# Fourteen more of block B's maximum reductions in the V stage, and the V rows stored from ScalarE's queue

## The chip, the cores and the metric

The kernel runs on one core of one Trainium2 chip. The metric is device time in microseconds (us) from launch to end, lower is better. Each kernel is run three times and the median counts; one more execution is profiled.

## The reference, cut to what matters

Two attention blocks over 2048 positions, width 640, 32 heads of 20 channels. Block A attends each position to 8 earlier positions at stride 2; block B is full softmax attention. The outputs stand side by side.

```python
def _B_ref(x, wqkv, wo):
    qkv = (x @ wqkv).reshape(B, S, 3, H, Dh).transpose(2, 0, 3, 1, 4)
    q, k, v = qkv[0], qkv[1], qkv[2]
    scores = jnp.einsum("bhqd,bhkd->bhqk", q, k) * (Dh ** -0.5)
    p = _softmax(scores, axis=-1)
    o = jnp.einsum("bhqk,bhkd->bhqd", p, v)
    return o.transpose(0, 2, 1, 3).reshape(B, S, D) @ wo
```

## The kernel before

The program is one long straight line of instructions. Its stages: block A's projections of q, k and v; block B's q and k projections; the **V stage**, block B's v projection; the **loop**, block B's attention; a tail without maxima; the last output projections. Block A's attention (pieces of GpSimd work, `a_attention`, line 350) runs under the later stages, one piece each time `next(a_work)` is called.

**PSUM.** One tile `ps_st` holds all 8 banks. `bank()` (line 115) hands out one bank, `wide()` (134) two neighbours. In the V stage banks 0 to 3 rotate for the projections, and the pairs 4-5 and 6-7 for the maxima. Inside the loop, `one` and `two` pick banks by estimated times while the order is written out.

**V stage** (lines 892 to 929). `V_GROUPS` has 32 groups, 30 of them here and the last two at the start of the loop. A group is 15 matmuls `128x320` into one bank (`rows15`, 263: weights `ww`, data `xn` and `xl`), a ScalarE copy into one of four row tiles `ve`, and a store of these rows to DRAM (`vb_d`). The store stands on SP's queue, one group later (`after(1, sp.dma_start, ...)`). Between the first groups SP also issues the loads of q (`bq`, four per group) on which the maxima rest, and after groups 8 and 16 loads of x.

**Maxima.** The softmax of block B needs each query's maximum over all keys before its exponentials. Work is counted in 512 *steps* (8 groups of 4 heads, 4 query blocks, 16 key blocks). One step of maxima is two halves; a half is a pair of matmuls (60 rows by 512 columns, side by side in the array, into a pair of banks: rows `ps_st<-bk,bq 60*128`) and a VectorE `tensor_reduce` of 128x1024. `b_max` (695) writes one step, and after groups 7 to 30 the V stage has one step each: 24 steps, `LEAD`. When 16 steps are done, `max_rows` (627) reduces and transposes them on VectorE and sends them into q's extra rows.

**Loop** (961 to 1015). Each `V` token ends a step: `begin` (DMA issues, block A's pieces) and `b_pv` (709: 8 recorded matmuls `ps_st<-e,vb` per step, and every second step a ScalarE copy). `S` writes two score halves (matmul `ps_st<-bq,bk 62*128`, ScalarE exponential of 128x512), `M` one half of maxima (two matmuls, one reduction of 1024), `Y` one score half beside half of a half of maxima (reduction of 512). The tokens stand in strings:

```python
PLAIN = "VYMSVYMSYY"                              # 2 steps, and 2 steps of maxima
MIXED = "VYMSVYjMYYFYMSYVYMSVYSMYVYkYSVMSY"       # 6 steps, block A's output piece at F
```

The loop runs 488 steps; its maxima are `LEAD` = 24 steps ahead, so the last 24 steps (the tail) have none. `i % 30 % 4 == 1` (line 974) says at which steps `i` below 240 block A takes its next piece.

Of the kernel before, what the change touches and what calls it, by code (L numbers as in the profile page):

```python
# [12 lines left out]
ALU = mybir.AluOpType  # L13
AX = mybir.AxisListType
# [10 lines left out]
VC = DH + 1  # L25
# [15 lines left out]
NKB = 16  # L41
NS = NG * NQC * NKB
LEAD = 24
LAG = 2
NEG = -1.0e30

# [19 lines left out]
def attention_pair(ctx, tc, xa, wqk_a, wv_a, wo_a, xb, wqk_b, wv_b, wo_b, oa, ob):  # L66
# [13 lines left out]
    def after(n, fn, *args):  # L80
        due.setdefault(now[0] + n, []).append((fn, args))
# [25 lines left out]

    psb = ps.tile([128, 8, 512], F32, name="ps_st")
    free = list(range(4))
    pair = [0]  # L110
    taken = {}
    read_at = []

# [19 lines left out]

    def wide():

        pair[0] += 1
        return psb[:, 4 + 2 * (pair[0] % 2):6 + 2 * (pair[0] % 2)]

    def one(t, *but):

# [48 lines left out]
    def chunk(t, xi, k):  # L189
        return t[k // (KC - 1)][:, xi, k % (KC - 1)]  # L190
# [69 lines left out]
        w = sb.tile([128, 2, KC, 128], F32R, tag="w", bufs=4, name="w")  # L260
        return w, [lambda: split(w[:, 0], w[:, 1], wqk_b[m])]

    def rows15(p, o, W):

        for k in range(KC):
            for i, (wi, xi) in enumerate(PASSES):
                pe.matmul(p[:, :320], o(xi, k), W[wi][:, k], start=(k == 0 and i == 0), stop=(k == KC - 1 and i == 2))

    def a_rows(p, x, t, g, W, ks, passes=PASSES):
        n = A_COLS[g + 1] - A_COLS[g]  # L270
# [402 lines left out]
    def max_tiles(i):  # L673
        u, sub = divmod(i, NKB)
        if sub == 0 and u not in mxt:
            mxt[u] = (sb.tile([128, 2, 8, 4], F32, tag="mx4", bufs=2, name="mx4"),
                      m1s[u % 2])
        return mxt[u]

    def m_matmul(i, j, r, p):  # L680

        u, sub = divmod(i, NKB)
        g, qc = divmod(u, NQC)
        q, k, v = stacks[g]
        pl, qb = divmod(sub // 2, 4)
        c = sub % 2 * 2 + j
        rows = slice(r * HALF, r * HALF + BS)
        pe.matmul(p, q[rows, qc, pl, qb * 128:qb * 128 + 128], k[rows, pl, c * 512:(c + 1) * 512], start=True, stop=True)

    def max_end(i):  # L690
        u, sub = divmod(i, NKB)
        if sub == NKB - 1:
            max_rows(*mxt[u], stacks[u // NQC][0], u % NQC)

    def b_max(i):

        m4 = max_tiles(i)[0]
        pq, ch = divmod(i % NKB, 2)
        for j in range(2):
            p = wide()  # L700
            for r in range(2):
                m_matmul(i, j, r, p[:, r])
            dve.tensor_reduce(m4[:, :, pq, 2 * ch + j], p, AX.X, ALU.max)
        max_end(i)

    P = {}
    accs, raws, spare = {}, {}, []
# [113 lines left out]
    def m_two():  # L821

        n = m_next[0]
        m_next[0] += 1
        max_tiles(n // 2 + LEAD)
        return "m", n // 2 + LEAD, n % 2

    def m_done(m):

# [59 lines left out]

    steps = iter(range(LEAD))
    WV = [WV, w1]
    groups = 0

    def v_group(n, half, s):
        p = bank()
        rows15(p, lambda xi, k: chunk(XB[n], xi, k)[:, s % 4 * 128:s % 4 * 128 + 128], WV[half])
        ve = ones[s % 4]
        act.copy(ve[:, :16 * VC].rearrange("p (h c) -> p h c", c=VC)[:, :, :DH],  # L900
                 p[:, :320].rearrange("p (h d) -> p h d", d=DH))
        give(p)
        c = 16 * VC + 11 * half
        after(1, sp.dma_start, vb_d[s * 128:(s + 1) * 128, half * 16 * VC:half * 16 * VC + c], ve[:, :c])


    V_GROUPS = [(n, half, s) for n in (2, 3, 0, 1) for half in range(2) for s in range(4 * n, 4 * n + 4)]
    v_late = V_GROUPS[-LAG:]
    for n, half, s in V_GROUPS[:-LAG]:
        v_group(n, half, s)  # L910
        tick()
        groups += 1
        if q_loads:
            for _ in range(4):
                q_loads.pop(0)()
        if groups == 1:
            wait[0] = 5
        if groups in (8, 16):
            XB[groups // 8 - 1], more = x_pieces(xb, groups // 8 - 1, gp)
            for fn in more:  # L920
                fn()
        if groups > 6:
            for i in islice(steps, 1):
                b_max(i)
        if groups > 16 and groups % 3 == 0 and groups != 21:
            next(a_work, None)
        if groups in (26, 28):
            v_piece(0, *((0, 4) if groups == 26 else (8, 16)))
# [31 lines left out]
    def begin(i):  # L960

        g, sub = divmod(i, NQC * NKB)
        if sub == 4 and g + 1 < NG:
            k_loads, q_loads = b_pieces(g + 1)
            for n, fn in enumerate(k_loads + q_loads + [lambda g=g + 1: v_piece(g, 0, NKB)]):
                after(1 + 2 * n, fn)
        if i in (NS - 56, NS - 40):
            out_first((i - NS + 56) // NKB)
        tick()
        if loads and i % 2:  # L970
            loads.pop(0)()
        if turn_jobs and turn_jobs[0][0] <= now[0]:
            run_jobs(turn_jobs, 1)
        if i > 14 and (i % 30 % 4 == 1 if i < 240 else i % 14 in (1, 5, 7, 11)):
            run_jobs(soft_jobs, 2)
            if next(a_work, 0) == 0:
                for d in done_a:
                    d[0] -= 1
        if done_a and done_a[0][0] <= 0:
            a_turn(*done_a.pop(0)[1:])  # L980
        turn_parts()


    PLAIN = "VYMSVYMSYY"
    MIXED = "VYMSVYjMYYFYMSYVYMSVYSMYVYkYSVMSY"
    i, order, mixed = 0, "", 0
    while i < NS - LEAD or order:
        if not order:
            if not left_a[0] and not WO_b:
                load_out(wo_b, WO_b)  # L990
            order = PLAIN
            if i + 6 <= NS - LEAD and ready_a and ready_a[0][0] <= now[0] + 3 and (
                    soft_jobs or next_a[0] == len(UNITS) or now[0] > max(mixed, ready_a[0][0]) + 14):
                order, mixed = MIXED, now[0] + 6
        kind, order = order[0], order[1:]
        if kind == "F":
            out_piece()
        elif kind == "j":
            run_jobs(*((soft_jobs, 1) if soft_jobs else (turn_jobs, 3)))
        elif kind == "k":  # L1000
            run_jobs(soft_jobs, 1)
            run_jobs(turn_jobs, KC)
        elif kind != "V":
            b_token(kind)
        else:
            begin(i)
            if i >= LAG:
                b_pv(i - LAG)
            else:
                v_group(*v_late.pop(0))  # L1010
                if not v_late:
                    load_out(wo_a, WO, (1,))

                    spare += [sb.tile([128, 2, 512], F32, tag="last0", bufs=2, name="more") for _ in range(2)]
            i += 1

    read_at.clear()
    for i in range(NS - LEAD, NS + LAG):
        begin(i)
        if i < NS:  # L1020
            b_qk(i)
        if i % 2:
            b_pv(i - LAG - 1)
            b_pv(i - LAG)
            if fill:
                fill.pop(0)()
# [57 lines left out]
```

## Time and profile before

| what | value |
|---|---|
| device time, median of 3 runs (lowest to highest) | 1791.26 us (1790.36 to 1794.95) |
| the profiled execution's own time / its span | 1788.76 us / 1787.0 us |
| granted TensorE clock, mean | 0.999 |
| busy share of the span: PE, PEld, DVE, ACT, POOL | 99%, 55%, 75%, 74%, 68% |
| V stage with maxima (364.9 to 437.0 us) | 24 steps of maxima |
| loop (437.0 to 1652.0 us) | 488 steps |

PE is TensorE's matmul, PEld its weight load, DVE VectorE, ACT ScalarE, POOL GpSimd, SPq the DMA issues of SyncE, ACTq those of ScalarE. A row of the timeline is one instruction or a run of equal ones: start, time from the start of the first to the end of the last, engine, line, operation, out<-in, count, and in brackets the idle time before it and what ended that. Neighbouring instructions overlap, so the distance between starts says more of their cost than their durations. Every row names line 61, the helper that records all instructions; names of tiles tell them apart.

### The profile page before, as it was taken

Reading aid. Unit: us, or ns where it says so; the run is one execution under the profiler, and the core shown is the slowest. Engines: PE = TensorE matmul, PEld = TensorE weight load, DVE = VectorE, ACT = ScalarE, POOL = GpSimd, SP = SyncE. Lnnn points to the kernel's source line nnn. Section 1 sums busy time; section 2 is a strip of 40 time slices with the busy share of each in tenths; the row PEclk is TensorE's granted clock in tenths of the full one; section 3 lists DMA queues with packets and bytes.
Section 4 is the critical chain, followed back from the end, with each engine's and each line's share of the span. In section 5 each row is a group of like instructions: output and inputs, shape, how many; then the busy total and the mean of one; then the engine's idle time right before and its main releaser. Section 6 shows DMA issues by size and latency. Waiting matters only on the chain. (4 is left out here: it accounts for less than half of the span.)

```text
span 1787.0 us, 31655 instructions
## 1 busy us (share of the span) xinstructions
PE 1772.1 (99%) x11211; PEld 987.1 (55%) x11211; DVE 1340.0 (75%) x1834; ACT 1327.2 (74%) x2593; POOL 1217.1 (68%) x1072
## 2 busy tenths in 40 slices
PE   9999999999999999999999999999999999999999
PEld 7988888887344444444444444444444434443469
DVE  3100232367999999999999999999999999999300
ACT  4222322222998999999999999998998998899881
POOL 0000069226679999989998999999999997337241
PEclk9999999999999999999999999999999999999999
DMA  6333696854535444354536336354444453113123
GB/s 228 116 100 102 190 304 245 270 187 139 152 88 148 124 136 120 106 151 133 147 99 170 96 113 163 121 159 130 133 142 124 122 149 94 30 44 86 32 70 114
DMA packets 191191, 240.22 MB, mean 134 GB/s; under 512 B 89020, under 2 KB 115260, under 8 KB 190040
## 3 DMA queue, kind: packets, MB, share of 16 engines
q1 hardware_dynamic: 190456, 237.54, 44.5%
q8 instruction: 88, 1.44, 0.4%
q14 instruction: 71, 0.58, 0.1%
q10 hardware_dynamic: 576, 0.66, 0.1%
HBM read 173.21 MB, written 64.91 MB: 133 GB/s over the span
## 5 line engine op out<-in xcount | busy, mean ns | idle before, releaser
L61 DVE TENSOR_REDUCE mx<-ps_st 128x1 f32<-128x512 f32 (+1 forms) x1512 | 1218.2, 871 | 57.7 <-PE ps_st L61 51.3
L61 ACT ACTIVATE e<-ps_st 128x512 f32<-128x512 f32 x2048 | 1066.2, 615 | 37.7 <-PE ps_st L61 16.4
L61 PE MATMUL ps_st<-bq,bk 62*128 62x512 f32 x2048 | 614.4, 436 | 1.4 <-DVE mx L61 0.6
L61 PE MATMUL ps_st<-bk,bq 60*128 60x512 f32 x2048 | 593.4, 446 | 3.9 <-DVE mx L61 2.1
L61 PEld LDWEIGHTS ps_st<-bq,bk 62*128 62x128 f32 x2048 | 283.0, 184 | 479.3 <-ACT e L61 282.3
L61 PE MATMUL ps_st<-e,vb 128*32 128x512 f32 x4096 | 543.7, 605 | 3.8 <-ACT e L61 2.6
L61 POOL TENSOR_TENSOR braw<-braw,more 128x512 f32<-128x512 f32 x224 | 287.8, 1285 | 136.5 <-ACT more L61 133.2
L61 POOL TENSOR_TENSOR akv<-akv,aq 128x1280 f32<-128x1280 f32 x64 | 189.0, 2953 | 234.4 <-DMA akv<-ka_d 234.4
L61 PEld LDWEIGHTS ps_st<-bk,bq 60*128 60x128 f32 x2048 | 267.7, 184 | 71.3 <-DVE mx L61 36.7
L61 POOL TENSOR_TENSOR akv<-akv 128x640 f32<-128x640 f32 (+3 forms) x304 | 282.2, 928 | 23.8
L61 ACT COPY ro<-ps_st 128x320 f32<-128x320 f32 (+2 forms) x124 | 61.2, 495 | 226.6 <-PE ps_st L61 177.2
L61 PEld LDWEIGHTS ps_st<-e,vb 128*32 128x32 f32 x4096 | 82.1, 108 | 158.8 <-ACT e L61 76.6
L61 POOL TENSOR_TENSOR akv<-akv,al 128x1280 f32<-128x1280 f32 x64 | 152.0, 2375 | 0.2
L61 ACT COPY more<-ps_st 128x512 f32<-128x512 f32 x224 | 133.4, 595 | 2.9 <-PE ps_st L61 2.7
L61 PE MATMUL ps_st<-wc,xn 128*128 128x512 f32 (+1 forms) x576 | 133.5, 376 | 0.4 <-ACT xn L61 0.4
L61 PE MATMUL ps_st<-ww,xn 128*128 128x320 f32 x768 | 125.8, 314 | 0.0
L61 PEld LDWEIGHTS ps_st<-ww,xn 128*128 128x128 f32 x768 | 113.4, 188 | 20.1 <-ACT ve L61 7.7
L61 PEld LDWEIGHTS ps_st<-wc,xn 128*128 128x128 f32 x576 | 106.2, 188 | 18.4 <-ACT xn L61 1.0
L61 PE MATMUL ps_st<-xn,w 128*128 128x512 f32 x480 | 115.7, 390 | 0.0
L61 PEld LDWEIGHTS ps_st<-xn,w 128*128 128x128 f32 x480 | 90.1, 188 | 19.4
L61 ACT CAST pr<-ps_st 128x512 fp32r<-128x512 f32 x40 | 23.5, 587 | 101.0 <-PE ps_st L61 101.0
L61 DVE TENSOR_TENSOR pr<-ps_st,pr 128x512 fp32r<-128x512 f32 x40 | 27.7, 692 | 91.7 <-ACT pr L61 91.7
(64 smaller groups left out, 986.0 us busy)
## 6 DMA issues: line engine op xcount, KB each, us to landing
akv<-ka_d SPq DMA_DIRECT2D x128, 320.0 KB
akv<-va_d SPq DMA_DIRECT2D x128, 320.0 KB
kb_d<-pr SPq DMA_DIRECT2D x20, 512.0 KB
qb_d<-pr SPq DMA_DIRECT2D x20, 512.0 KB
bk<-kb_d SPq DMA_DIRECT2D x16, 640.0 KB
bq<-qb_d SPq DMA_DIRECT2D x64, 160.0 KB
rb<-s_d SPq DMA_DIRECT2D x128, 64.0 KB
stg<-xb SPq DMA_DIRECT2D x12, 512.0 KB
```

The source lines that it names most:

```text
L61: return self.tc.keep_in_program_order(op(*a, **k))
```

## The change

1. `LEAD_0` = 31: the V stage computes 31 steps of maxima (62 halves) instead of 24 (48 halves), and the loop's maxima begin at step 31. They no longer stand between groups but inside them: `behind` is called after each of a group's matmuls, and three halves are written after matmul 105 of the stage and then after every 17th (21 places, the last with two halves).
2. PSUM: the maxima rotate over three pairs (2-3, 4-5, 6-7). The first six groups use banks 6, 4, 7, 5, 1, 0, and from group 7 on groups alternate between banks 1 and 0.
3. The V rows' store follows its copy at once on ScalarE's queue; the two late groups in the loop still use SP.
4. In the loop a third string, `LIGHT`, has 6 steps and 5 steps of maxima. It is taken in place of `PLAIN` seven times from step 16 on, wherever `MIXED` is not due, and brings the lead back from 31 to 24.
5. At step 61 block A's piece is left out; the pieces behind it all come one place later.

```diff
--- before.py
+++ after.py
@@ -41,6 +41,7 @@
 NKB = 16
 NS = NG * NQC * NKB
 LEAD = 24
+LEAD_0 = 31
 LAG = 2
 NEG = -1.0e30
 
@@ -107,7 +108,7 @@
 
     psb = ps.tile([128, 8, 512], F32, name="ps_st")
     free = list(range(4))
-    pair = [0]
+    pair, pairs_at = [0], [4, 2]
     taken = {}
     read_at = []
 
@@ -133,8 +134,9 @@
 
     def wide():
 
-        pair[0] += 1
-        return psb[:, 4 + 2 * (pair[0] % 2):6 + 2 * (pair[0] % 2)]
+        first, n = pairs_at
+        pair[0] = (pair[0] + 1) % n
+        return psb[:, first + 2 * pair[0]:first + 2 * pair[0] + 2]
 
     def one(t, *but):
 
@@ -260,11 +262,12 @@
         w = sb.tile([128, 2, KC, 128], F32R, tag="w", bufs=4, name="w")
         return w, [lambda: split(w[:, 0], w[:, 1], wqk_b[m])]
 
-    def rows15(p, o, W):
+    def rows15(p, o, W, behind=lambda n: None):
 
         for k in range(KC):
             for i, (wi, xi) in enumerate(PASSES):
                 pe.matmul(p[:, :320], o(xi, k), W[wi][:, k], start=(k == 0 and i == 0), stop=(k == KC - 1 and i == 2))
+                behind(3 * k + i + 1)
 
     def a_rows(p, x, t, g, W, ks, passes=PASSES):
         n = A_COLS[g + 1] - A_COLS[g]
@@ -692,16 +695,16 @@
         if sub == NKB - 1:
             max_rows(*mxt[u], stacks[u // NQC][0], u % NQC)
 
-    def b_max(i):
+    def b_max(i, j):
 
         m4 = max_tiles(i)[0]
         pq, ch = divmod(i % NKB, 2)
-        for j in range(2):
-            p = wide()
-            for r in range(2):
-                m_matmul(i, j, r, p[:, r])
-            dve.tensor_reduce(m4[:, :, pq, 2 * ch + j], p, AX.X, ALU.max)
-        max_end(i)
+        p = wide()
+        for r in range(2):
+            m_matmul(i, j, r, p[:, r])
+        dve.tensor_reduce(m4[:, :, pq, 2 * ch + j], p, AX.X, ALU.max)
+        if j:
+            max_end(i)
 
     P = {}
     accs, raws, spare = {}, {}, []
@@ -822,8 +825,8 @@
 
         n = m_next[0]
         m_next[0] += 1
-        max_tiles(n // 2 + LEAD)
-        return "m", n // 2 + LEAD, n % 2
+        max_tiles(n // 2 + LEAD_0)
+        return "m", n // 2 + LEAD_0, n % 2
 
     def m_done(m):
 
@@ -889,24 +892,39 @@
 
 
 
-    steps = iter(range(LEAD))
+    steps = iter(range(2 * LEAD_0))
     WV = [WV, w1]
     groups = 0
 
+    maxima_at = {7 * 15 + n * 17 for n in range(21)}
+
+    def maxima(n):
+        if groups * 15 + n in maxima_at:
+            for m in islice(steps, 3):
+                b_max(*divmod(m, 2))
+
     def v_group(n, half, s):
         p = bank()
-        rows15(p, lambda xi, k: chunk(XB[n], xi, k)[:, s % 4 * 128:s % 4 * 128 + 128], WV[half])
+        rows15(p, lambda xi, k: chunk(XB[n], xi, k)[:, s % 4 * 128:s % 4 * 128 + 128], WV[half], maxima)
         ve = ones[s % 4]
         act.copy(ve[:, :16 * VC].rearrange("p (h c) -> p h c", c=VC)[:, :, :DH],
                  p[:, :320].rearrange("p (h d) -> p h d", d=DH))
         give(p)
         c = 16 * VC + 11 * half
-        after(1, sp.dma_start, vb_d[s * 128:(s + 1) * 128, half * 16 * VC:half * 16 * VC + c], ve[:, :c])
+        dst = vb_d[s * 128:(s + 1) * 128, half * 16 * VC:half * 16 * VC + c]
+        if read_at:
+            after(1, sp.dma_start, dst, ve[:, :c])
+        else:
+            act.dma_start(dst, ve[:, :c])
 
 
     V_GROUPS = [(n, half, s) for n in (2, 3, 0, 1) for half in range(2) for s in range(4 * n, 4 * n + 4)]
     v_late = V_GROUPS[-LAG:]
+
+    free[:], pairs_at[:], pair[0] = [6, 4, 7, 5, 1, 0], [2, 3], 0
     for n, half, s in V_GROUPS[:-LAG]:
+        if groups == 6:
+            free[:] = [1, 0]
         v_group(n, half, s)
         tick()
         groups += 1
@@ -919,9 +937,6 @@
             XB[groups // 8 - 1], more = x_pieces(xb, groups // 8 - 1, gp)
             for fn in more:
                 fn()
-        if groups > 6:
-            for i in islice(steps, 1):
-                b_max(i)
         if groups > 16 and groups % 3 == 0 and groups != 21:
             next(a_work, None)
         if groups in (26, 28):
@@ -971,7 +986,7 @@
             loads.pop(0)()
         if turn_jobs and turn_jobs[0][0] <= now[0]:
             run_jobs(turn_jobs, 1)
-        if i > 14 and (i % 30 % 4 == 1 if i < 240 else i % 14 in (1, 5, 7, 11)):
+        if i > 14 and (i % 30 % 4 == 1 and i != 61 if i < 240 else i % 14 in (1, 5, 7, 11)):
             run_jobs(soft_jobs, 2)
             if next(a_work, 0) == 0:
                 for d in done_a:
@@ -981,9 +996,11 @@
         turn_parts()
 
 
+
     PLAIN = "VYMSVYMSYY"
+    LIGHT = "YYSVYYYVYMYSVYYYVSMSYVYMSVYY"
     MIXED = "VYMSVYjMYYFYMSYVYMSVYSMYVYkYSVMSY"
-    i, order, mixed = 0, "", 0
+    i, order, mixed, fewer = 0, "", 0, LEAD_0 - LEAD
     while i < NS - LEAD or order:
         if not order:
             if not left_a[0] and not WO_b:
@@ -992,6 +1009,9 @@
             if i + 6 <= NS - LEAD and ready_a and ready_a[0][0] <= now[0] + 3 and (
                     soft_jobs or next_a[0] == len(UNITS) or now[0] > max(mixed, ready_a[0][0]) + 14):
                 order, mixed = MIXED, now[0] + 6
+            elif i > 14 and fewer:
+                order = LIGHT
+                fewer -= 1
         kind, order = order[0], order[1:]
         if kind == "F":
             out_piece()
@@ -1015,6 +1035,7 @@
             i += 1
 
     read_at.clear()
+    free[:], pairs_at[:], pair[0] = [0, 1, 2, 3], [4, 2], 0
     for i in range(NS - LEAD, NS + LAG):
         begin(i)
         if i < NS:
```

**TensorE in the V stage, about the first maxima.** Before:

```order
L61 MATMUL ps_st<-ww,xl 128x320 x3
L61 MATMUL ps_st<-bk,bq 128x512 x4
L61 MATMUL ps_st<-ww,xn 128x320 x12
L61 MATMUL ps_st<-ww,xl 128x320 x3
L61 MATMUL ps_st<-bk,bq 128x512 x4
```

and now:

```order
L62 MATMUL ps_st<-ww,xl 128x320 x3
L62 MATMUL ps_st<-bk,bq 128x512 x6
L62 MATMUL ps_st<-ww,xn 128x320 x12
L62 MATMUL ps_st<-ww,xl 128x320 x3
L62 MATMUL ps_st<-ww,xn 128x320 x2
L62 MATMUL ps_st<-bk,bq 128x512 x6
L62 MATMUL ps_st<-ww,xn 128x320 x10
L62 MATMUL ps_st<-ww,xl 128x320 x3
L62 MATMUL ps_st<-ww,xn 128x320 x4
L62 MATMUL ps_st<-bk,bq 128x512 x6
```

Two halves after every 15 matmuls became three halves after every 17, so the places wander through the groups.

**SP's queue at the first loads of q.** The names in brackets are the semaphores that an instruction waits for; the eight DMAHW ones are shared by the DMAs of all queues in turn, and a DMA waits until the one that last counted on its semaphore has landed. Before:

```order
L61 DMA vb_d<-ve 128x336 [waits DMAHW4_49,Activation_49]
L61 DMA bq<-qb_d 20x1024 [waits DMAHW5_49,PE_49]
L61 DMA bq<-qb_d 40x1024 [waits DMAHW6_49]
L61 DMA bq<-qb_d 20x1024 [waits DMAHW7_49]
L61 DMA bq<-qb_d 40x1024 [waits DMAHW0_49]
L61 DMA vb_d<-ve 128x336 [waits DMAHW1_49,Activation_49]
```

and now, with the V rows' stores on ScalarE's queue:

```order
L62 DMA bk<-kb_d 22x4096 [waits DMAHW1_49]
L62 DMA bq<-qb_d 20x1024 [waits DMAHW3_49,PE_49]
L62 DMA bq<-qb_d 40x1024 [waits DMAHW4_49]
L62 DMA bq<-qb_d 20x1024 [waits DMAHW5_49]
L62 DMA bq<-qb_d 40x1024 [waits DMAHW6_49]
L62 DMA bq<-qb_d 20x1024 [waits DMAHW7_49]
```

SP no longer waits for ScalarE here. But semaphores 4, 5 and 6, for which the second to fourth load of q wait, are now those of the stores of V groups 3, 4 and 5 on ScalarE's queue.

**VectorE in the loop** (128x1 is a reduction of 512, 128x2 one of 1024; the number behind `mx` is a buffer's). Before, in `PLAIN` steps:

```order
L61 TENSOR_REDUCE mx_3488<-ps_st 128x1
L61 TENSOR_REDUCE mx_3488<-ps_st 128x2
L61 TENSOR_REDUCE mx_3488<-ps_st 128x1 x3
L61 TENSOR_REDUCE mx_3488<-ps_st 128x2
L61 TENSOR_REDUCE mx_3488<-ps_st 128x1
```

and now, in a `LIGHT` stretch:

```order
L62 TENSOR_REDUCE mx_3756<-ps_st 128x1
L62 TENSOR_REDUCE mx_3756<-ps_st 128x2
L62 TENSOR_REDUCE mx_3756<-ps_st 128x1 x4
L62 TENSOR_REDUCE mx_3756<-ps_st 128x2
L62 TENSOR_REDUCE mx_3756<-ps_st 128x1 x2
L62 TENSOR_REDUCE mx_3756<-ps_st 128x2
L62 TENSOR_REDUCE mx_3756<-ps_st 128x1 x8
```

Per 2 steps there were 2 wide and 4 narrow reductions; per 6 steps there are now 3 wide and 14 narrow instead of 6 and 12.

## Rows read from the trace of the kernel before

**Rows 1.** The page, busy time and share of the span by engine.
```profile
PE 1772.1 (99%) x11211; PEld 987.1 (55%) x11211; DVE 1340.0 (75%) x1834; ACT 1327.2 (74%) x2593; POOL 1217.1 (68%) x1072
```
**Rows 2.** Busy time in stretches: the V stage, and five of the loop.
```profile
core 0: us, PE busy (x) PEld busy (x) DVE busy (x) ACT busy (x) POOL busy (x), PEclk, DMA share, GB/s
366.58:436.98 70.40, 70.40 (x438) 57.54 (x437) 54.92 (x50) 15.55 (x32) 37.89 (x32) 1.00 0.52 155
...
463.65:477.86 14.21, 14.13 (x96) 5.74 (x96) 14.18 (x19) 13.81 (x28) 7.67 (x8) 1.00 0.54 159
544.66:566.99 22.33, 22.33 (x154) 8.90 (x154) 22.21 (x33) 21.70 (x44) 21.39 (x23) 1.00 0.63 175
477.86:536.55 58.69, 57.68 (x385) 23.45 (x384) 58.55 (x82) 55.64 (x110) 46.88 (x37) 1.00 0.31 88
552.86:566.99 14.13, 14.13 (x97) 5.86 (x96) 14.01 (x18) 13.77 (x28) 13.58 (x13) 1.00 0.59 162
582.93:611.77 28.84, 28.34 (x194) 11.61 (x192) 28.54 (x37) 28.02 (x57) 27.58 (x28) 1.00 0.37 108
```
**Rows 3.** The second stretch of the loop, the value matmuls alone.
```profile
544.66:566.99 22.33, 10.56 (x80) 1.48 (x80) 1.00 0.63 175
```
**Rows 4.** Timeline of PE and DVE about one V group with maxima.
```profile
384.30 0.73 PE L61 MATMUL ps_st<-bk,bq 60*128 60x512 f32 x4
384.84 2.36 DVE L61 TENSOR_REDUCE mx<-ps_st 128x2 f32<-128x1024 f32 x2 [0.70 <-PE ps_st L61]
387.36 0.50 PE L61 MATMUL ps_st<-bk,bq 60*128 60x512 f32 x2
```
**Rows 5.** Groups by form: the wide reduction.
```profile
L61 DVE TENSOR_REDUCE mx<-ps_st 128x2 f32<-128x1024 f32 x536 | 649.9, 1216 | 33.0 <-PE ps_st L61 32.8
```
**Rows 6.** Timeline of DVE in the V stage: its other work there.
```profile
414.84 0.22 DVE L61 TENSOR_REDUCE mx<-mx 128x16 f32<-128x64 f32 x1
415.47 2.36 DVE L61 TENSOR_REDUCE mx<-ps_st 128x2 f32<-128x1024 f32 x2 [0.16 <-PE ps_st L61]
429.95 0.34 DVE L61 RECIPROCAL am<-am 128x32 f32<-128x32 f32 x1
```
**Rows 7.** Timeline of PE, ACT and SP, first V groups to first maxima.
```profile
351.02 1.91 PE L61 MATMUL ps_st<-ww,xn 128*128 128x320 f32 x12
351.95 0.33 SPq L61 DMA_DIRECT2D vb_d<-ve  x1
353.21 1.92 PE L61 MATMUL ps_st<-ww,xn 128*128 128x320 f32 x12
363.77 0.43 ACT L61 COPY ve<-ps_st 128x320 f32<-128x320 f32 x1 [5.55 <-DMA vb_d<-ve]
364.89 0.47 PE L61 MATMUL ps_st<-bk,bq 60*128 60x512 f32 x1 [0.56 <-DMA bq<-qb_d]
365.92 0.73 PE L61 MATMUL ps_st<-bk,bq 60*128 60x512 f32 x3 [0.56 <-DMA bq<-qb_d]
```
**Rows 8.** Timeline of PE, ACT and DVE in PLAIN steps of the loop.
```profile
470.45 1.08 ACT L61 ACTIVATE e<-ps_st 128x512 f32<-128x512 f32 x2
471.52 0.58 ACT L61 COPY more<-ps_st 128x512 f32<-128x512 f32 x1
472.00 4.25 ACT L61 ACTIVATE e<-ps_st 128x512 f32<-128x512 f32 x8
473.15 1.06 PE L61 MATMUL ps_st<-e,vb 128*32 128x512 f32 x8
474.14 0.50 PE L61 MATMUL ps_st<-bq,bk 62*128 62x512 f32 x1
474.72 0.40 PE L61 MATMUL ps_st<-bq,bk 62*128 62x512 f32 x2
475.05 1.07 PE L61 MATMUL ps_st<-e,vb 128*32 128x512 f32 x8
```
**Rows 9.** Timeline of ACT at the kernel's end: an issue on its queue.
```profile
1781.43 0.38 ACTq L61 DMA_DIRECT2D ob<-ro  x1
```

## The prediction

> **What bounds the kernel now.** The page comes first: TensorE is busy for 99% of the span [rows 1], but its matmul records overlap, so this share alone does not say that TensorE sets the pace. The busy times by stretch [rows 2] do. In `PLAIN` steps of the loop VectorE is busy for 14.18 of 14.21 us, ScalarE for 13.81: six steps (96 TensorE records, 16 per step) at 2.37 us each, paced by VectorE. In another stretch ten steps (80 value matmuls, 8 per step [rows 3]) took 22.33 us, 2.23 each, with ScalarE busy for 21.70 us and TensorE without a gap [rows 2]: that is the fastest that the loop shows with these engines side by side. In the V stage VectorE is busy for 54.92 of 70.40 us [rows 2]; there TensorE sets the pace, and before each place with maxima VectorE stands idle for 0.70 us [rows 4]. So the change takes reductions from a stage in which VectorE is the limit to one in which it has 15 us to spare, and TensorE carries the same matmuls in either stage.
>
> A rule that would read this otherwise: the Trainium skill (Trainium Kernel Development and Optimization, Performance Expectations) calls matmul busy time a bad metric and weight-load busy time a good one. Weight loads are busy for 5.74 of 14.21 us in the `PLAIN` stretch [rows 2], which agrees that TensorE is not the limit there; were the 99% taken as the limit, the loop would give back only the 28 matmuls, 14 pairs at 0.29 us (below), 4.1 us.
>
> **V stage, TensorE.** A group of 15 matmuls alone takes 353.21 - 351.02 = 2.19 us [rows 7], 0.146 per matmul. With two halves behind it, it takes 387.36 - 384.30 = 3.06 [rows 4], so a place with two halves costs 0.87. A third half: one pair of matmuls lasts 0.50 and two last 0.73 [rows 4], so 0.23; in the loop neighbouring pairs stand (474.72 - 474.14) / 2 = 0.29 apart [rows 8], the dearer bound. I take 0.23, the row of the same stage, so 1.10 per place. Behind the first place there were 23 places, 23 x 0.87 = 20.0 us; now there are 19 of three halves and one of two, 19 x 1.10 + 0.87 = 21.8. With the third half of the first place the stage grows by 2.0 us.
>
> **V stage, VectorE.** Two reductions take 2.36 us where one takes 1.22 [rows 4, 5], so they start 1.14 apart. Three per place need 3.42; places stand 17 x 0.146 + 1.10 = 3.58 apart. VectorE keeps up with 0.16 to spare, but no longer with room for its other work: the block maximum and its transpose push the next reduction by 415.47 - 414.84 = 0.63, a reciprocal takes 0.34 [rows 6]. With three pairs of banks TensorE's third half waits for the reduction of the third half of the place before, so most of these 0.97 us become TensorE's wait: I take 0.8. Together the stage grows by **2.8 us**; the bounds are 2.0 (no wait) and 2.0 + 0.97 + 19 x 0.06 = 4.1 (every third half at the loop's distance, all other work waited for).
>
> **V stage, queues and banks.** SP loses 30 issues; ScalarE gains 30 of 0.38 us [rows 9], in a stage in which it is busy for 15.55 of 70.40 us [rows 2]: hidden. Were ScalarE late, its copies would free banks late, and with two banks for the groups TensorE waits as soon as a copy is later than one group. At the start of the maxima TensorE waited twice for loads of q, 0.56 us each [rows 7]. The loads come no sooner now: their semaphores are shared with the stores of V groups 3 to 5, and the last of these cannot be issued before its copy at about 360.5 us (351.02 + 4 x 2.19, and the copy). I take no change here. Below, both waits go: -1.1. Above: a store issued at 351.95 let go of its tile only when a copy, 5.55 us late, went on at 363.77 [rows 7], 11.5 us later. If V stores still need that, the fourth load of q is issued at 372.0 and not before, 6.1 us after TensorE had its data at 365.92: +6.1.
>
> This is where a rule of the Trainium skill weighs against the row: by DMA: Bandwidth & Descriptors (Queues, rings and completion order) SP and ScalarE each own a ring on the same 16 DMA engines, and an engine goes round between rings. Then a store on ScalarE's ring would pass the bulk loads that SP has queued, and the +6.1 would shrink towards nothing. No row here shows two queues busy at once.
>
> **Loop.** Seven `LIGHT` strings are 42 steps: 24 in a row, 6 behind the first `MIXED`, 12 behind the second. The same steps before took 58.69 + 14.13 + 28.84 = 101.7 us [rows 2]. What a light step needs: VectorE, with 3 wide and 14 narrow reductions per 6 steps, (3 x 1.14 + 14 x 0.61) / 6 = 1.99 us, where a narrow one costs (14.21 / 3 - 2 x 1.14) / 4 = 0.61 of a pair of `PLAIN` steps. ScalarE, unchanged, four exponentials and half a copy of 512 columns; a copy's start stands 472.00 - 471.52 = 0.48 before the next [rows 8], so 4.5 x 0.48 = 2.16. TensorE: value matmuls and the switch to them, 0.99 + 0.33, and 16 further pairs at 0.29 per 6 steps [rows 8], 2.09. VectorE falls out as the limit; ScalarE comes next, TensorE close behind. So a light step lies between 2.16 and the 2.37 of a `PLAIN` step. I take 2.26: the fastest stretch, 2.23 [rows 2, 3], in which the same two engines were full, and a little for VectorE's backlog at the start of each light run. 42 x 2.26 = 94.9: **-6.7 us**; the bounds are 42 x 2.16 = 90.7, -10.9, and 0.
>
> **The piece left out.** GpSimd is busy for 46.88 of 58.69 and 27.58 of 28.84 us in these steps [rows 2]; at 2.26 us per step it would have less time for the same pieces, and one piece less covers about what is lost. The pieces behind it come 4 steps, some 10 us, later, and block A's last output with them; the tail's weights for block B's output are loaded behind it, well ahead of the tail. Price: nothing, since the last `MIXED` string ends 22 steps, some 50 us, before the tail needs what follows it. Were that cover gone, the tail would wait for at most the 10 us.
>
> **Sum.** +2.8 - 6.7 = -3.9. The profiled execution took 1788.8 us and would take 1784.9. The median of the three runs is 1791.3, 2.5 above it; on the median I predict **1787.4 us**.
>
> **The rivals.**
> - *Light steps run at ScalarE's floor.* For it: the exponentials need nothing but free banks, and five in six of VectorE's bank holds remain. Against: TensorE's 2.09 has no slack for waits. With 2.18 per step, 91.6, the loop gives back 10.1; with a V stage of +2.0 to +2.8 the time is about 1783.6.
> - *The stores hold up the first maxima (slower).* V stores on ScalarE's queue land as late as those on SP's did, the shared semaphores pass this on to the loads of q, and TensorE stands still for 6.1 us at its first maxima; behind it two banks instead of four leave no slack for the late copies, another 1 to 2. It decides as soon as the stores take over 8 us to land. -3.9 + 6.1 + 1.5: about 1795.0.
> - *The light steps are not faster.* VectorE's place is taken at once by TensorE, whose pairs wait for banks that ScalarE holds, and the steps stay near 2.36. Against: the stretch at 2.23. The V stage's +2.8 alone is left: 1794.1. This is also what it comes to if the change moved the reductions without relieving the loop.
>
> **How the numbers follow.** A measurement of this kernel tells about 0.3%, 5.4 us, from no change: faster is below 1785.9, slower above 1796.7. The forecast case (light steps of 2.22 to 2.30, V stage +2 to +4) has 0.62, and a sixth of it lies below 1785.9; ScalarE's floor 0.22, all of it faster; the late stores 0.09, half of it slower; no relief 0.07, within 0.3%. Faster: 0.10 + 0.22 = 0.32. Slower: 0.04. The same: 0.64. The forecast case alone spans 1785 to 1790. The range that leaves out 2 in 10 reaches down to the floor case, 1782.5, and up to just short of the late stores, 1793.
>
> **What would show it.** In the V stage: VectorE busy over 95%, 17 wide reductions per 20 us instead of 13 or 14, places 3.6 us apart, the first loop group 3 us later than 437.0. In the light runs: 2.26 us per step, ScalarE busy over 95%, VectorE below 92%. From step 70 on the same pace as before, with `MIXED` strings 4 steps later, and the end some 4 us earlier. I am wrong if the wait at the first maxima grows by more than 2 us, if TensorE waits at most places for VectorE (places 3.8 us apart would cost 4 us more), if light steps stay above 2.33, or if GpSimd's work comes late enough to make VectorE wait for it.

## The result, and the profile after

The changed kernel takes 1797.64 us, the median of 7 runs (1795.80 to 1798.83), where the kernel before, run beside it, takes 1790.99 us (1788.82 to 1794.95, 7 runs). The ratio is 1.0040 with a 95% interval of 1.0031 to 1.0049: slower by 6.65 us in the medians, above the predicted range. The profiled execution took 1798.12 us, with a span of 1796.2 us and a mean granted TensorE clock of 0.996.

The page's first part, busy time by engine, hardly moves [rows 1]:

```profile
PE 1770.3 (99%) x11211; PEld 987.3 (55%) x11211; DVE 1342.1 (75%) x1841; ACT 1324.9 (74%) x2593; POOL 1218.4 (68%) x1072
```

So the 9.2 us between the two spans are idle time and a lower clock, in few places. To find them, the table takes from the timelines, one profiled execution of each kernel, where the value matmuls (`ps_st<-e,vb`, 8 per step) of a step start, and gives for the change, and for the experiments below, how many us later than in the kernel before that is. The medians come from four sessions, in which the kernel before itself took 1789.92 to 1790.99 us, so differences of 1 us between medians of different sessions say little; e1 to e4, e5 to e8 and e9 to e12 share a session each.

| kernel | step 0 | step 68 | step 380 | step 404 | step 511 | median, us |
|---|---|---|---|---|---|---|
| before (start, us) | 444.42 | 611.77 | 1398.46 | | 1738.37 | 1789.9 to 1791.0 |
| the change | +10.61 | +5.11 | +4.95 | +10.80 | +9.17 | 1797.64 |
| e1: stores on SP's queue | +6.02 | +0.54 | -0.07 | +6.44 | +4.91 | 1794.25 |
| e2: piece at 61 taken | +9.13 | +3.46 | +5.48 | +8.97 | +7.38 | 1796.48 |
| e3: both | +4.11 | -1.58 | -1.36 | +0.06 | +0.32 | 1790.59 |
| e4: before, stores on ScalarE's queue | +7.62 | +7.58 | +7.21 | +9.57 | +9.70 | 1797.53 |
| e5: first stores on GpSimd's queue | +7.47 | +2.00 | +3.05 | +8.58 | +6.99 | 1796.02 |
| e9: late piece two steps later | +11.48 | +5.97 | +6.23 | +9.32 | +7.77 | 1798.12 |
| e10: e3, other banks | +5.72 | +0.07 | +0.41 | +1.94 | +2.21 | 1792.09 |
| e11: e10, late piece at 401 | +3.53 | -2.17 | -1.84 | -2.47 | -3.85 | 1787.49 |

Three moves show for the change: 10.6 us lost by step 0, 5.5 won up to step 68, where the light steps are, and 5.85 lost between steps 380 and 404. Some 1.6 come back before step 488, and they are no gain of the change: early in the tail the clock fell to 0.50 for 3.4 us in the profile of the kernel before and not in that of the change. Before, then the change:

```profile
1670.30:1673.70 3.40, 3.40 (x19) 1.34 (x21) 0.42 (x2) 3.31 (x8) 0.46 (x2) 0.50 0.19 58
```

```profile
1681.00:1684.40 3.40, 3.40 (x28) 1.58 (x26) 0.43 (x2) 3.19 (x7) 0.46 (x2) 1.00 0.20 54
```

It falls there in some profiles (also e3, e10 and e12) and not in others (also e1 and e11), so the table's columns for steps 404 and 511 can differ by some 1.5 us from this alone.

**The first loss: the first maxima.** The timeline of TensorE in the change:

```profile
363.88 0.60 PE L62 MATMUL ps_st<-ww,xl 128*128 128x320 f32 x3
367.90 0.47 PE L62 MATMUL ps_st<-bk,bq 60*128 60x512 f32 x1 [3.42 <-DMA vb_d<-ve]
371.65 1.61 PE L62 MATMUL ps_st<-bk,bq 60*128 60x512 f32 x5 [3.29 <-DMA bq<-qb_d]
373.19 3.00 PE L62 MATMUL ps_st<-ww,xn 128*128 128x320 f32 x12
376.85 0.97 PE L62 MATMUL ps_st<-bk,bq 60*128 60x512 f32 x6
...
441.81 0.99 PE L62 MATMUL ps_st<-bk,bq 60*128 60x512 f32 x6
```

Two waits of 0.56 us [rows 7] have become 3.42 and 3.29, and the V groups go on at 373.19 where they went on at 366.58. The chain of waits over these microseconds names the links (start, duration, what was waited for):

```profile
354.01 8.52 DMA vb_d<-ve
...
362.55 0.02 ACTq L62
...
362.61 3.71 DMA vb_d<-ve
...
366.65 0.33 SPq L62
...
367.40 4.21 DMA bq<-qb_d
...
371.65 4.39 PE ps_st L62 x16
```

A V store issued on ScalarE's queue at 354.01 lands 8.52 us later. Only then is a later store issued, at 362.61; it takes 3.71 us, and only behind it does SP go on with the loads of q. The load that TensorE needs is issued at 367.40 and takes 4.21 us more.

The busy times by stretch show the rest: the V stage from the end of that wait, the three light runs (24, 6 and 12 steps), and two stretches at a granted clock of 0.50.

```profile
core 0: us, PE busy (x) PEld busy (x) DVE busy (x) ACT busy (x) POOL busy (x), PEclk, DMA share, GB/s
373.19:447.60 74.41, 73.89 (x465) 61.17 (x464) 71.08 (x65) 15.20 (x30) 38.78 (x33) 0.99 0.44 141
...
488.48:543.16 54.68, 54.64 (x371) 21.66 (x369) 51.64 (x81) 54.34 (x111) 43.99 (x36) 1.00 0.36 106
559.00:573.10 14.10, 14.09 (x94) 5.76 (x93) 12.99 (x20) 14.01 (x29) 13.55 (x12) 1.00 0.68 188
589.05:616.89 27.84, 27.83 (x188) 10.94 (x186) 25.30 (x36) 27.65 (x57) 26.63 (x25) 1.00 0.34 113
...
368.60:375.40 6.80, 3.75 (x13) 3.06 (x14) 2.88 (x3) 0.00 (x0) 0.00 (x0) 0.50 0.50 170
1454.00:1460.80 6.80, 4.79 (x20) 1.94 (x20) 5.39 (x7) 2.73 (x5) 6.72 (x6) 0.50 0.59 210
```

The V stage takes 74.41 us from there on, 4.0 more than before [rows 2]. About 1 us of that is the clock: TensorE ran at 1.2 GHz from 368.60 to 375.40, and twelve V matmuls took 3.00 us at 373.19. In the light steps VectorE no longer sets the pace (busy for 94%, 92% and 91%). ScalarE is busy for 54.34 of 54.68 and 27.65 of 27.84 us and is the likely next limit; TensorE's records leave as little (54.64 and 27.83), and no run tells the two apart. The 42 light steps take 96.62 us where the same steps took 101.66 before [rows 2], and nearly all of the gain is in the run of 24, 54.68 for 58.69.

**The second loss: GpSimd near 1450 us.** The timeline of GpSimd and VectorE before:

```profile
1431.54 2.96 POOL L61 TENSOR_TENSOR akv<-akv,aq 128x1280 f32<-128x1280 f32 x1
...
1438.45 0.60 DVE L61 TENSOR_REDUCE am<-al 128x32 f32<-128x256 f32 x1 [0.84 <-POOL al L61]
```

and of GpSimd, VectorE and TensorE in the change:

```profile
1447.38 2.95 POOL L62 TENSOR_TENSOR akv<-akv,aq 128x1280 f32<-128x1280 f32 x1
1450.40 3.40 POOL L62 TENSOR_TENSOR akv<-akv 128x640 f32<-128x640 f32 x4
1453.88 0.32 POOL L62 TENSOR_TENSOR al<-akv 128x64 f32<-128x64 f32 x1
1454.23 0.59 DVE L62 TENSOR_REDUCE am<-al 128x32 f32<-128x256 f32 x1 [5.97 <-POOL al L62]
1456.01 0.80 PE L62 MATMUL ps_st<-bq,bk 62*128 62x512 f32 x2 [5.42 <-DVE mx L62]
1456.73 1.94 PE L62 MATMUL ps_st<-e,vb 128*32 128x512 f32 x8
```

VectorE comes to the maximum of block A's last softmax (`am<-al`) while GpSimd is still at the piece that makes `al`. VectorE's reductions behind it wait, TensorE finds no bank for 5.42 us, and then its clock is 0.50 for 6.8 us: eight value matmuls take 1.94 us, not 1.06 [rows 8]. GpSimd starts this piece 15.8 us later than before, while the loop stands some 5 us later: the difference is about the four steps by which the left-out piece moves the others.

### The profile page after: what moved, and what is told of

Same layout as the page of the kernel before. It is cut to its first block, busy times and chain, and to the rows that moved or that the text cites. A ratio compares the mean times of both kernels' runs of the same rounds, so it can differ in the third digit from the quotient of the medians.

```text
span 1796.2 us, 31658 instructions
## 1 busy us (share of the span) xinstructions
PE 1770.3 (99%) x11211; PEld 987.3 (55%) x11211; DVE 1342.1 (75%) x1841; ACT 1324.9 (74%) x2593; POOL 1218.4 (68%) x1072
## 4 chain that ended last, share of the span: by engine, by line
PE 82%; DVE 9%; POOL 3%; DMA 2%; ACT 1%; issue 1%; SPq 0%; POOLq 0%; DVEq 0%; ACTq 0%
PE ps_st L62 82%; DVE mx L62 9%; POOL akv L62 2%; ACT e L62 1%; POOL braw L62 1%; DMA vb_d<-ve 1%; DMA oa<-ro 1%; DMA s_d<-braw 0%; POOL aot L62 0%; DMA bq<-qb_d 0%; DMA mdr<-mtr 0%; DMA akv<-ka_d 0%; DMA akv<-va_d 0%; POOL al L62 0%; ACT more L62 0%
```

## The experiments

Theory at the start: the stores' queue costs the first loss, the piece left out the second, and the moved maxima are worth about what was predicted. Rival: the moved maxima themselves cost it.

**e1: the V stores back on SP's queue.**

```diff
-        if read_at:
-            after(1, sp.dma_start, dst, ve[:, :c])
-        else:
-            act.dma_start(dst, ve[:, :c])
+        after(1, sp.dma_start, dst, ve[:, :c])
```

> The change with the V rows' stores back on SP's queue; all else as in the change. Theory A (on ScalarE's queue the stores hold up the first loads of q, through the DMA semaphores that both queues share, and TensorE stands still for 6.7 us at its first maxima): the two waits there fall to about the 1.1 us of before, the clock does not drop there, and the time falls by about 7 us, from 1797.6 to about 1790.5. Rival A' (the loads of q are late because the DMA engines are full of bulk loads, whichever queue carries the V rows): the waits stay above 5 us and the time above 1796.

Measured: 1794.25 us (1791.88 to 1796.86, 10 runs), ratio to before 1.0025 (1.0015 to 1.0034). The wait for loads at the first maxima is gone, but the seventh V group now waits for a bank, and the clock falls all the same. The timeline of TensorE, and the busy times about the wait:

```profile
364.68 3.51 PE L62 MATMUL ps_st<-ww,xn 128*128 128x320 f32 x12 [2.77 <-ACT ve L62]
...
368.56 0.96 PE L62 MATMUL ps_st<-bk,bq 60*128 60x512 f32 x6
```

```profile
364.00:368.00 4.00, 3.32 (x12) 3.32 (x13) 0.00 (x0) 0.85 (x2) 0.00 (x0) 0.57 0.63 203
```

This is what the banks of the first groups cost, as e10 shows below: ScalarE's copy waits for an old store to let go of its row tile, and with four banks [rows 7] TensorE did not feel it. The wait near 1450 us stays, at 6.4 us. Undoing the queue gives back 3.4 us by the medians, and 2.3 if each is measured beside its own kernel before; 7 were expected.

**e2: the piece at step 61 taken again.**

```diff
-        if i > 14 and (i % 30 % 4 == 1 and i != 61 if i < 240 else i % 14 in (1, 5, 7, 11)):
+        if i > 14 and (i % 30 % 4 == 1 if i < 240 else i % 14 in (1, 5, 7, 11)):
```

> The change with block A's piece at step 61 back in its place. Theory G (the piece left out moves every later piece one place on, so that the last softmax's maximum meets a gap of 2 steps where it had more, and VectorE waits 6.0 us for GpSimd near 1450 us): that wait falls to about the 0.8 us of before and the time by about 6 us, to about 1791. Rival G' (GpSimd is late because the light steps give it less time): the wait stays, or comes earlier and longer, and the time stays at 1797 or rises.

Measured: 1796.48 us (1793.78 to 1798.67, 6 runs), 1.0036 (1.0024 to 1.0048). The late wait falls from 5.97 to 2.2 us, but a new one stands near 640 us, just behind the light steps: GpSimd, with a piece more to do, is late with the row maxima for q's extra rows. The table of waits and the timeline:

```profile
DVE am L62 <- POOL al L62: 2.2, 1, 2.2
PE ps_st L62 <- DMA bq<-mdr: 1.7, 1, 1.7
```

```profile
643.78 0.76 PE L62 MATMUL ps_st<-bq,bk 62*128 62x512 f32 x1 [1.73 <-DMA bq<-mdr]
...
645.36 1.92 PE L62 MATMUL ps_st<-e,vb 128*32 128x512 f32 x8
```

So the left-out piece does spare a wait behind the light steps (0.7 us there in the change), and pays for it 800 us later. That putting it back gives only 1.2 us by the medians, and 0.1 if each is measured beside its own kernel before, fits neither the 6 us of the theory nor, with the late wait down by 3.8 us, its rival.

**e3: both undone; the maxima, the banks and the light steps are left.**

> Both undone: what is left is the 14 maxima in the V stage, the banks, and the light steps. Theories A and G: neither long wait, about 1784 to 1785, some 6 us under the kernel before (light steps -5.7 against the V stage's +3 and what the clock gives). Rivals A' and G': 1796 to 1798. If only one of the theories holds: about 1791.

Measured: 1790.59 us (1788.65 to 1793.81, 10 runs), 1.0006 (0.9996 to 1.0016): no change. Against e2, undoing the queue is worth 5.9 us; against e1, undoing the left-out piece 3.7. The light steps win 5.7 us (step 0 to 68) and the V stage loses 4.1. Here TensorE waits 2.25 us for the copy at the first maxima, and its clock does not fall:

```profile
364.22 2.03 PE L62 MATMUL ps_st<-ww,xn 128*128 128x320 f32 x12 [2.25 <-ACT ve L62]
```

**e4: the kernel before, with its V stores on ScalarE's queue at once and nothing else changed.**

```diff
-        after(1, sp.dma_start, vb_d[...], ve[:, :c])
+        if read_at:
+            after(1, sp.dma_start, dst, ve[:, :c])
+        else:
+            act.dma_start(dst, ve[:, :c])
```

> The kernel before with this one part of the change: the V rows' stores on ScalarE's queue. Theory A: TensorE waits some 6 to 7 us at its first maxima and the time rises from 1791 to about 1797. Rival A': no difference, 1791.

Measured: 1797.53 us (1795.86 to 1798.83, 6 runs), 1.0040 (1.0028 to 1.0053). The queue alone makes the kernel before 7.6 us slower, no less than the whole change. The timeline of TensorE shows the same pair of waits with four banks, so the banks are not their cause:

```profile
367.60 0.76 PE L61 MATMUL ps_st<-bk,bq 60*128 60x512 f32 x1 [3.35 <-DMA vb_d<-ve]
370.80 1.19 PE L61 MATMUL ps_st<-bk,bq 60*128 60x512 f32 x3 [2.43 <-DMA bq<-qb_d]
371.91 3.56 PE L61 MATMUL ps_st<-ww,xn 128*128 128x320 f32 x12
```

The 7.6 us stay to step 380. Then comes the late wait again, 2.1 us and a low clock, with the pieces in their old places: GpSimd starts the piece for it 8.5 us later than before (1440.04 for 1431.54) and the loop stands only 7.2 later. So the wait can come back without the left-out piece; what held GpSimd back was not traced.

**e5: the first seven groups' stores on GpSimd's queue,** whose transfers count on other semaphores than the eight that SP's and ScalarE's share (the section on the change says that all queues share them; GpSimd's does not). It tells whether the loads of q wait for the stores or are slow by themselves.

```diff
-            act.dma_start(dst, ve[:, :c])
+            (gp if groups < 7 else act).dma_start(dst, ve[:, :c])
```

> The change, with the V rows of the first seven groups stored from GpSimd's queue, whose transfers count on semaphores of their own. Theory (shared semaphores: SP's loads of q wait until the V stores that last counted on their semaphore have landed): the loads of q are issued as the program reaches them, TensorE's waits before the first maxima fall from 3.42 + 3.29 us to at most 2 in all, its clock stays near 1.0 there, step 0 of the loop stands +3 to +5 us against the kernel before instead of +10.6, and the time falls by 6 to 8 us, to about 1790. The wait of VectorE for GpSimd near 1450 us stays, 5 to 6.5 us. Rival (the transfers themselves are slow under the bulk loads of these microseconds, whatever queue and semaphore): the waits stay at 5 us or more and the time at 1796 to 1798. Second rival (GpSimd, which issues the stores, is itself late at them): the copies wait for their row tiles instead, 2 to 3 us, and the time is near 1793.

Measured: 1796.02 us (1795.58 to 1799.02, 7 runs), 1.0030 (1.0019 to 1.0041): 1.6 below the change by the medians and 0.6 if each is measured beside its own kernel before, not 6 to 8. The waits fall from 6.71 to 2.65 us, and SP issues the first six loads of q between 351.64 and 355.6, where the first stood at 360.06 in the change. So the loads did wait for the stores, although the time lies in the range of the rival. The stores themselves are slow on this queue too: 5.1 to 9.4 us from issue to landing, only that no load waits for them. Timeline of TensorE, the chain of waits up to its last row, and the busy times behind the waits:

```profile
366.10 0.47 PE L62 MATMUL ps_st<-bk,bq 60*128 60x512 f32 x1 [1.69 <-DMA bq<-qb_d]
367.53 1.62 PE L62 MATMUL ps_st<-bk,bq 60*128 60x512 f32 x5 [0.96 <-DMA bq<-qb_d]
369.08 3.57 PE L62 MATMUL ps_st<-ww,xn 128*128 128x320 f32 x12
```

```profile
350.52 14.10 DMA bk<-kb_d
...
364.63 2.84 DMA bq<-qb_d
```

```profile
368.00:372.00 4.00, 4.00 (x16) 3.29 (x14) 3.49 (x3) 0.00 (x0) 0.00 (x0) 0.50 0.48 171
```

What is left of the wait is the next transfer in line: a load of k rows issued at 350.52 takes 14.10 us, and a load of q that needs its semaphore is issued the moment it lands. And the clock falls as in the change. Step 0 gains 3.1 us, of which the runs keep half at most.

**e6, e7, e8: the left-out piece taken at step 9,** where the kernel takes none (`if i == 9 or i > 14 and (...)`), with the stores on SP's queue (e6), on GpSimd's for seven groups (e7), and on SP's with four loads of q ahead of the V groups (e8).

> The change, with the V stores back on SP's queue, and with the piece that is left out at step 61 taken at step 9 of the loop instead, where the kernel before takes none. Theory (the wait near 1450 us comes from the order of block A's pieces, which the missing piece shifts by one, and the wait near 640 us that putting it back brings comes from too little GpSimd time in the light steps): both waits go, VectorE's near 1450 us falls from 6.4 to under 2.5 us, TensorE's for the row maxima near 640 us from 1.5 to under 0.5, and the time is 1787 to 1789.5, 1 to 3 us below the change with both parts undone (1790.6) and 5 to 7 below that with the queue alone undone (1794.3). Rival (any piece more in the first hundred steps makes GpSimd late somewhere): a wait of 1.5 us or more appears at steps 9 to 60 or stays near 640, and the time is 1790 to 1792.

> The change, with the first seven groups' V rows stored from GpSimd's queue and the left-out piece taken at step 9. If both theories hold, each part gives what it gives alone: no wait above 2 us at the first maxima, none above 2.5 near 1450, none near 640; the loop's light steps then show in the end, and the time is 1784 to 1787, the fastest of all so far. If the first maxima still wait: 1791 to 1794. If only the piece fails: 1788 to 1790.

> As the kernel with SP's queue and the piece at step 9, and the first four loads of q issued ahead of the V groups' stores. Theory (the loads wait for stores that last counted on their semaphore): with no store ahead of them, the loads are issued before 361 us, TensorE has no wait for q at its first maxima, and step 0 stands 1 to 3 us nearer to the kernel before than without that edit (+4 to +6 with the stores on SP): 1785.5 to 1788. Rival (ScalarE's late copies, with two banks for the groups, set the pace of the first places, and the loads hide behind them): no gain, within 1 us of the kernel without the edit.

Measured: e6 1793.98 us (1791.44 to 1796.12, 11 runs), e7 1794.24 (1792.17 to 1795.98, 11 runs), e8 1796.85 (1794.43 to 1797.81, 7 runs); all above every range that their expectations named. In e6 the wait near 640 us goes (0.7 us), as expected, but the late one is still 3.2 us: with the maxima of the softmax in their old place, two pieces of block A's output (0.72 and 1.56 us on GpSimd) now stand ahead of it. In e7 no single wait is long (1.67 and 0.90 us at the first maxima, 2.4 for the late one), and yet the clock falls in both places, and once more in the tail. In e8 the early loads push the V stores back, a copy comes 8.34 us late and TensorE waits 4.90 us for it: what the loads gain the stores lose, in the same microseconds.

**e9: the change, with one late piece two steps later.**

```diff
-... else i % 14 in (1, 5, 7, 11)):
+... else i % 14 in (1, 5, 7, 11) and i != 399 or i == 401):
```

> The change, with one of block A's late pieces taken at step 401 instead of 399, the one ahead of which VectorE takes block A's last maximum. Theory (the missing piece at step 61 moves this maximum from a place that lies four steps behind GpSimd's piece to one that lies two steps behind it, and GpSimd needs about 8 us for a piece, more than two steps): VectorE's wait for GpSimd near 1450 us falls from 5.97 us to at most 1.5, TensorE's clock stays at 1.0 there, the loop gains 4 to 6 us between steps 390 and 420, and the time falls to 1791.5 to 1794. Rival (GpSimd is behind in any case, and the wait only moves to the next piece): VectorE waits 4 us or more within the next ten steps, and the time stays at 1796 to 1798.

Measured: 1798.12 us (1795.54 to 1798.22, 5 runs), 1.0041 (1.0028 to 1.0054): no gain. The wait did fall, from 5.97 to 1.66 us, and did not move elsewhere; but the clock falls behind the short wait as behind the long one. Timeline of VectorE and TensorE:

```profile
1455.01 0.60 DVE L62 TENSOR_REDUCE am<-al 128x32 f32<-128x256 f32 x1 [1.66 <-POOL al L62]
1456.26 0.79 PE L62 MATMUL ps_st<-bk,bq 60*128 60x512 f32 x1 [1.60 <-DVE mx L62]
1456.98 1.94 PE L62 MATMUL ps_st<-e,vb 128*32 128x512 f32 x8
```

By the table the step from 380 to 404 costs 3.09 us where it cost 5.85. That this does not show in the time is partly a later step 0 (0.87 us; the clock there stayed down to 377.2 us, in the change to 375.4), and a span that ends 1.5 us later behind step 511 than the change's: at 1789.20 the issue of an output store on ScalarE's queue took 2.19 us where the others there take 0.34, and ScalarE's last three copies followed late.

**e10, e11, e12: other banks, and the late piece at 401 instead of 397.** e10 is e3 with banks 3 and 2 for the fifth and sixth V group, so that no late copy holds the seventh's; e11 adds the moved piece; e12 is e11 with the piece of step 61 at step 9.

```diff
-    free[:], pairs_at[:], pair[0] = [6, 4, 7, 5, 1, 0], [2, 3], 0
+    free[:], pairs_at[:], pair[0] = [6, 4, 7, 5, 3, 2], [2, 3], 0
...
-... else i % 14 in (1, 5, 7, 11)):
+... else i % 14 in (1, 5, 7, 11) and i != 397 or i == 401):
```

> The kernel with both parts undone (V stores on SP's queue, piece at step 61 taken), and banks 3 and 2 instead of 1 and 0 for the fifth and sixth V group, so that the seventh and eighth have banks that no late copy holds. Theory (what is left of the wait at the first maxima, 2.3 to 2.9 us, is the late copies' hold on banks 1 and 0): TensorE has no wait for a copy there, the first maxima come 1.5 to 2.5 us earlier, near 364.5 to 365, step 0 of the loop stands +1.5 to +2.6 us against the kernel before instead of +4.1, and the time is 1788 to 1789.5 where the kernel without the edit took 1790.6. Rival (the copies are late whichever bank they free, and the third half of the first maxima, in banks 2 and 3, waits for them instead): the wait moves by one matmul run, step 0 stands at +3.5 to +4.5, and the time is 1790 to 1791.

> As the kernel with SP's queue and the other banks, and block A's late piece at step 397 taken at 401, so that its last maximum lies six steps behind the piece it needs. Theory: VectorE's wait for GpSimd near 1440 us, 2.3 us with both parts undone, goes to under 0.5, worth 1 to 2 us: 1786.5 to 1788.5. Rival: the wait is covered by VectorE's slack there, no gain, within 0.7 us of the kernel without this edit.

> SP's queue, the other banks, the late piece at 401 instead of 397, and the piece of step 61 taken at step 9. Theory (three separate waits, each with its own cure): no wait over 1.5 us at the first maxima, near 640 us or near 1440 us, TensorE's clock at 1.0 in all three, step 0 at +2 to +3, step 68 at -3 to -4, and the end as much ahead of the kernel before: 1786 to 1788. Rival (the early piece makes GpSimd late elsewhere, as the extra 1.5 us behind step 440 in the kernel with the piece at step 9 hints): 1789 to 1791.

Measured: e10 1792.09 us (1788.64 to 1793.28, 11 runs), 1.0008 (0.9999 to 1.0017); e11 1787.49 (1784.30 to 1791.03, 11 runs), 0.9984 (0.9975 to 0.9993); e12 1789.12 (1785.47 to 1790.27, 11 runs), 0.9991 (0.9982 to 1.0000). The wait for copies falls to 0.6 us or less in all three. What is left are the loads of q, and here e10 and e11, which are the same program up to the loop, differ. Timeline of TensorE in e10:

```profile
365.32 0.46 PE L62 MATMUL ps_st<-bk,bq 60*128 60x512 f32 x1 [0.83 <-DMA bq<-qb_d]
366.60 1.25 PE L62 MATMUL ps_st<-bk,bq 60*128 60x512 f32 x5 [0.82 <-DMA bq<-qb_d]
367.78 2.90 PE L62 MATMUL ps_st<-ww,xn 128*128 128x320 f32 x12
```

and in e11, with VectorE's late maximum, which waits no longer:

```profile
364.22 0.46 PE L62 MATMUL ps_st<-bk,bq 60*128 60x512 f32 x1
365.26 0.70 PE L62 MATMUL ps_st<-bk,bq 60*128 60x512 f32 x3 [0.58 <-DMA bq<-qb_d]
366.18 0.50 PE L62 MATMUL ps_st<-bk,bq 60*128 60x512 f32 x2 [0.22 <-ACT ve L62]
366.60 2.03 PE L62 MATMUL ps_st<-ww,xn 128*128 128x320 f32 x12
...
1440.28 0.62 DVE L62 TENSOR_REDUCE am<-al 128x32 f32<-128x256 f32 x1
```

Transfers that come a microsecond later made 2.2 us at step 0, since the clock fell in one profile and not in the other: the twelve V matmuls take 2.90 us for 2.03. e11 is the only kernel clearly below the one before: 2.8 us by the medians measured side by side, 0.16%, and some 10 below the change. In its profile 1.3 of the 3.85 us at step 511 are the clock in the tail, which did not fall, and 0.6 lie between steps 380 and 404, where its piece was moved. So 14 maxima moved are worth a little, about the 1.8 us of step 380, once nothing else waits. e12's gain up to step 404 is given back behind it (-3.73 to -1.06), with the clock in the tail falling as in the kernel before; why was not traced.

## Why the prediction was wrong

- **The step that failed** is "V stage, queues and banks": "I take no change here". It saw the link from the stores of groups 3 to 5 to the loads of q by their semaphores, put the issue of the last of these stores at about 360.5 us, and took from this that the loads come no sooner and no later. What counts is when the stores land: 8.52 us after its issue for the one at 354.01, and the next one of the chain was issued only then, at 362.61. The V groups went on 6.6 us later, 5.6 of it the longer waits (6.71 for 1.12), just above the upper end that the same paragraph had worked out, +6.1. That the two lie so close is partly luck: the +6.1 ends at the issue of the load and leaves out the 4.21 us that it takes, and it has one store of 11.5 us where the chain has two, of 8.52 and 3.71. The prediction put its own slower rival at 0.09, and that is what happened; e4 shows it by itself and e5 shows that the loads waited for the stores.
- **The rival's price** was 1795.0 and the time 1797.64. Beyond its 6.1 there was the clock (about 1 us) and the second loss, which it did not hold; the 1 to 2 us that it added for late copies came to 0.5 in the change.
- **The rule weighed against the row.** By the Trainium skill (DMA: Bandwidth & Descriptors, Queues, rings and completion order) SP and ScalarE have a ring each, and a DMA engine takes them in turn. The prediction read from this that a store on ScalarE's ring would pass SP's backlog, and the trace agrees in part: 8.52 us where a store on SP's queue took 11.5. It did not shrink the wait, because the loads of q then queued behind the stores by the semaphores.
- **The piece left out** was priced at "nothing", with the tail as the only reader of its lateness. The reader that mattered was VectorE, in whose row of reductions the softmax's maximum stands: 5.97 us of wait, then the low clock. The last line of what would make the prediction wrong named it; the sum did not. By itself, taking the piece again gives 0.1 to 1.2 us (e2; the ranges of runs overlap), beside the undone queue 3.7 (e3 against e1). Part of this wait is not the piece's: e4, with all pieces in place, has 2.1 us of it.
- **The V stage's own growth** was right: places 3.61 us apart (376.85 to 441.81 in 18) where 3.58 were forecast, VectorE busy for 71.08 of 74.41 us, and +4.0 us in all, about 1 of it the clock, where +2.8 was forecast.
- **The light steps** were right in that VectorE fell out as the limit, and a little short in size: 5.0 us in the three runs, 5.5 between steps 0 and 68 (5.7 in e3), for the predicted 6.7. The run of 24 came out at 2.28 us per step for the forecast 2.26; the six steps behind the first `MIXED` gave nothing (14.10 us for 14.13). Which engine is the next limit stays open.
- **Banks.** "With two banks for the groups TensorE waits as soon as a copy is later than one group" was written and not priced. e1 and e3 show it at 2.77 and 2.25 us; it lay hidden in the change behind the longer wait for q.

## What to carry to other kernels

Before a transfer is moved to another queue, list what waits for its landing, semaphores that later transfers share with it included, and price it by landing time, not by issue. A small gain that rests on three full engines is lost to the first waits of 2 to 6 us: the pieces that cross engines (here GpSimd's maximum in VectorE's order) need their distance counted in steps of the slowest of them whenever anything in that order shifts. Cures are to be tried together as well as apart, since each of these waits hid another.

## What the runs showed of the hardware

TensorE's granted clock went from 1.0 to 0.50, 2.4 to 1.2 GHz, not only at the long waits (3.42 us and 5.42 us in the change) but also at 1.60 us alone in e9, at 1.73 in e2 and behind 0.83 + 0.82 in e10. It stayed up at 2.25 us in e3. At one and the same place in the tail it fell in e3, e10 and e12 behind waits of 1.42 to 1.43 us, and stayed up in the change and in e11 behind 1.47 and 1.46: the length of a wait alone does not tell whether it falls.

In the change it stayed down for 6.8 us both times. Of what that cost, 0.97 us stand on the twelve V matmuls (3.00 against e11's 2.03) and 0.88 on the eight value matmuls of a step. Cutting a wait from 5.97 to 1.66 us (e9) left this part of the loss as it was.

A load of k rows took 14.10 us from issue to landing (e5), a store of V rows 8.52 and a load of q 4.21 (the change), all between 350 and 372 us: which of them is late moves from one kernel to the next.
